# Reordering the first loads and the start of the weight loads in a linear-attention and soft-mixture kernel

## The chip, the core and the metric

The kernel runs on one core of a Trainium2 chip. The metric is the time on the device in microseconds (us); the median of several runs is given. A profile of one execution stands beside it; its span is shorter than the measured time by some 2 us, since it begins with the first instruction.

## What is computed

A linear attention with decay (batch 4, 8 heads, sequence 768, head width 48), whose output goes through a soft mixture of 8 experts with 4 slots each.

```python
state = np.zeros((B, H, D, D))
for t in range(S):
    kt, vt, rt = k[:, :, t], v[:, :, t], r[:, :, t]
    cur = einsum('bhd,bhe->bhde', u[None] * kt, vt)
    y[:, :, t] = einsum('bhd,bhde->bhe', rt, state + cur)
    state = w[None, :, :, None] * state + einsum('bhd,bhe->bhde', kt, vt)
x = y.transpose(0, 2, 1, 3).reshape(B * S, H * D)      # 3072 x 384

logits = x @ phi                                        # phi: 384 x 32
d = exp(logits - logits.max(0)); d /= d.sum(0) + 1e-9   # over the tokens
slot_input = (d.T @ x).reshape(E, 4, 384)
for e in range(8):
    slot_out[e] = relu(slot_input[e] @ w1[e]) @ w2[e]   # 384x1024, 1024x384
c = exp(logits - logits.max(1)); c /= c.sum(1) + 1e-9   # over the slots
out = c @ slot_out.reshape(32, 384)
```

Everything arrives and leaves as float32. r, k and v have 4.7 MB each, the expert weights 25.2 MB together, the output 4.7 MB.

## The kernel before

The attention works in chunks of 128 positions. A loop over `i` from -5 to 31 runs over half sequences of pairs of heads, as a software pipeline: in one pass different stages belong to different pairs. The decay is applied by powers of `w`, made from `Ln` and `Exp` on ScalarE out of one row, `w_row`.

The loads of r, k and v go through the queue of the sync engine (SP), in the order of the program:

```python
O(dve.memset(wu[:], 1.0))
O(sp.dma_start(out=w_row, in_=w.rearrange("(o h) d -> o (h d)", o=1)))
O(act.preload_act_table_set("natural_log_exp_and_others"))
O(act.dma_start(out=wu3[0:4, :, 0:D], in_=...))   # w again, for the transposed form
O(act.dma_start(out=wu3[4:8, :, 0:D], in_=...))   # u
...
load_batch(0, 2)          # k, r, v of two heads at a time, through SP
load_batch(1, 2)
O(sp.dma_start(out=phi_f, in_=...))
load_batch(2, H)          # k, r, v of all heads at a time
...
def spread(bank, a, z):   # w_row to all partitions by TensorE, then its logarithm
    O(pe.matmul(bank[:, 0:z - a], one_f, w_row[:, a:z], start=True, stop=True))
    O(act.activation(out=lnw[:, a:z], in_=bank[:, 0:z - a], func=AF.Ln))
```

There are three raw buffers for four batches; the fourth batch takes the buffer of the first, and its loads stand in the loop at `i == 3`. The expert weights go through GpSimd's queue, which also turns them from float32 into bfloat16 on the way. The `w1` have a buffer of their own, the `w2` take the raw buffers of the second and third batch once these are read. GpSimd also makes the products of k and r with the powers of the decay (`scale`). The loads of the weights are dealt over the loop; the first of them stands behind a small copy, `guard`, that reads the last batch's k and so keeps the weights behind it:

```python
W_AT = {13: 1, 14: 1, 15: 1, 16: 1, 18: 1, 19: 1, 20: 1, 22: 1, 23: 1, 25: 1, 26: 5}
for i in range(-5, nH):
    ...                                            # TensorE, VectorE, ScalarE stages
    if odd and 0 <= mu + 3 < nU:
        scale(mu + 3, 0)                           # GpSimd: k times decay
    if not odd and 0 <= mu + 2 < nU:
        scale(mu + 2, 1)                           # GpSimd: r times decay
    ...
    if i == 3:
        load_kr(0, k, B - 1, 0, H)                 # last batch
        load_kr(1, r, B - 1, 0, H)
        for h0 in range(0, H, 2):
            load_v(B - 1, h0, h0 + 2)
    if i == 5:
        O(act.copy(phi_b[:], phi_f))
    ...
    if i == min(W_AT):
        O(pool.tensor_copy(guard[:], raw_of(0, B - 1)[:, 0:1]))
    for _ in range(W_AT.get(i, 0)):
        load_w(nw)                                 # w1 of expert 0..7, then w2
        nw += 1
for y0, y1 in ((0, 4), (4, 6), (6, 8)):            # the last w2 in three pieces of rows
    load_w(nw, y0, y1)
```

After the loop the slots' inputs go through both layers of the experts. The second layer works expert by expert at its end and, within an expert, row by row, so that it can begin with the pieces of the last `w2` that are there:

```python
def second(g, experts):
    for y in range(nF):                            # 8 rows
        for x in range(2):
            for j in experts:
                O(pe.matmul(SO[x][32 * j:32 * j + 32, :], hT[g][:, y, 32 * j:32 * j + 32],
                            w2_of(g * EG + j)[:, y, x * HD:(x + 1) * HD], ...))
...
second(1, (EG - 2,))
second(1, (EG - 1,))                               # the last expert
row_sums(8, 12)
so = cst.tile([128, Dm], bf, name="so")            # slot outputs, divided by the sums
...                                                # out = c @ so, in 24 tiles, and the stores
```

Of the kernel before, what the change touches and what calls it, by code (L numbers as in the profile page):

```python
# [9 lines left out]
def kernel(  # L10
# [16 lines left out]
    Nn, Dm = out.shape  # L27
    ES = moe_phi.shape[1]
    E = moe_w1.shape[0]
    F = moe_w1.shape[2]  # L30
    Spe = ES // E
    nM = Dm // C
# [14 lines left out]
    bf = mybir.dt.bfloat16  # L47
# [4 lines left out]
    def O(ins):  # L52
        return tc.keep_in_program_order(ins)

    pe, dve, act, pool, sp = nc.tensor, nc.vector, nc.scalar, nc.gpsimd, nc.sync

    big = ctx.enter_context(tc.tile_pool(name="big", bufs=1))
    cst = ctx.enter_context(tc.tile_pool(name="cst", bufs=1))
# [36 lines left out]
    w_row = early[0:1, 0:H * D]  # L95
# [5 lines left out]
    phi_f = late[:, 128:128 + nM * ES]  # L101
    wu = cst.tile([8, 128], f32, name="wu")
    wu3 = wu[:].rearrange("q (e s) -> q e s", s=64)
    O(dve.memset(wu[:], 1.0))
    O(sp.dma_start(out=w_row, in_=w.rearrange("(o h) d -> o (h d)", o=1)))
    O(act.preload_act_table_set("natural_log_exp_and_others"))
    O(act.dma_start(out=wu3[0:4, :, 0:D], in_=w.rearrange("(q e) d -> q e d", e=2)))
    O(act.dma_start(out=wu3[4:8, :, 0:D], in_=u.rearrange("(q e) d -> q e d", e=2)))
# [104 lines left out]
    ones = cst.tile([128, 128], bf, name="ones")  # L213
    Le_t = [cst.tile([128, L, 128], bf, name=f"Le{j}") for j in range(2)]
    phi_s = cst.tile([128, nM, ES], bf, name="phi_s")
    phi_b = cst.tile([128, nM * ES], bf, name="phi_b")
    assert JV == nM
    acc = cst.tile([128, NA], f32, name="acc")
    guard = cst.tile([128, 1], f32, name="guard")
    st = {}  # L220

# [56 lines left out]
    def v_pe(i):  # L278
        m, b, q, g, n = at(i)
        vb = st["vb", m]  # L280
        for c in range(L):
            for j in range(JV):
                o = C * c - j + JV - 1
                O(pe.matmul(Vb[:, c * P2:(c + 1) * P2], Q3[:, o:o + C], vb[:, :, g, j, :],  # L284
                            start=(j == 0), stop=(j == JV - 1)))
# [6 lines left out]
    def a_pe(i):  # L292
        m, b, q, g, n = at(i)
        kT, rT = st["kT", m], st["rT", m]
        for c in range(L):
            t = slice((g * L + c) * C, (g * L + c + 1) * C)
            for e in range(2):
                s = slice(64 * e, 64 * e + 64)
                O(pe.matmul(Ab[:, e, c * C:(c + 1) * C], kT[s, t], rT[s, t]))  # L299

    def mask_f(i):
        AT = wk.tile([128, 2, L, C], bf, name="AT", bufs=2)
        st["AT", i] = AT
        O(dve.tensor_mul(AT[:], Ab[:, :, 0:T].rearrange("p e (c t) -> p e c t", c=L),  # L304
                         mask_ut[:, None, None, :].to_broadcast([128, 2, L, C])))
# [62 lines left out]
    def y_evac(i):  # L368
        m, b, q, g, n = at(i)
        if q == 0:  # L370
            st["x", n] = wk.tile([128, L, Dm], bf, name="x", bufs=4)
        O(act.copy(st["x", n][:, :, q * P2:(q + 1) * P2],  # L372
                   Yb[:, 0:L * P2].rearrange("p (c e) -> p c e", c=L)))
# [31 lines left out]
    def le_t(n, lp=None):  # L405
        Le = st["Le", n]
        lp = le_p if lp is None else lp
        for c in range(L):
            O(pe.transpose(lp[:, c * C:(c + 1) * C], Le[:, c, :], ident[:]))

    def let_ev(n, lp=None, eng=None):
        lp = le_p if lp is None else lp
        if eng is dve:
            O(dve.tensor_copy(LexpT[:, n * T:(n + 1) * T], lp))
        else:
            O(act.copy(LexpT[:, n * T:(n + 1) * T], lp))

    def disp(n, ds_p, first=True):
        x, Le = st["x", n], st["Le", n]
        for mi in range(nM):  # L420
            for c in range(L):
                O(pe.matmul(ds_p[:, mi * ES:(mi + 1) * ES].rearrange("p (j x) -> p j x", j=EG), x[:, c, mi:Dm:nM],
                            Le[:, c, :].rearrange("p (j x) -> p j x", x=32)[:, :, 0:2 * Spe],
                            start=(first and mi == 0 and c == 0), stop=(c == L - 1), skip_group_check=True))
        for c in range(L):
            O(pe.matmul(ds_p[:, NA - 1:NA], Le[:, c, :], ones[:, 0:1],
                        start=False, stop=(c == L - 1), skip_group_check=True))

    def disp_ev(n, ds_p):
        if n == 0:  # L430
            O(dve.tensor_copy(acc[:], ds_p))
        else:
            O(dve.tensor_add(acc[:], acc[:], ds_p))
# [28 lines left out]
            xt_ev(*ch[s])  # L462

    pend = []
    W_AT = {13: 1, 14: 1, 15: 1, 16: 1, 18: 1, 19: 1, 20: 1, 22: 1, 23: 1, 25: 1, 26: 5}
    T_AT = {-4: [(tt, 0, 1), (tt, 1, 1), (ex, 0, 1), (tt, 0, 2)], -3: [(ex, 1, 1), (ex, 0, 2)],
            -1: [(tt, 1, 2), (ex, 1, 2)], 0: [(tt, 0, 3), (ex, 0, 3)], 1: [(tt, 1, 3), (ex, 1, 3)]}
    Z_AT = {-3: 0, -1: 1, 1: 2, 2: 3}
# [2 lines left out]
    Wf = [t[:].rearrange("p q j d -> p (q j d)") for t in W]  # L471
# [3 lines left out]
    def turn(n, blocks, bank, eng):  # L475
        x, w_ = st["x", n], L * len(blocks) * C
        for b, mi in enumerate(blocks):
            for c in range(L):
                o = (b * L + c) * C
                O(pe.transpose(bank[:, o:o + C], x[:, c, mi * C:(mi + 1) * C], ident[:]))  # L480
        dst = xs[:, n - n0, blocks[0]:blocks[-1] + 1].rearrange("p m c t -> p (m c t)")
        if eng is dve:
            O(dve.tensor_copy(dst, bank[:, 0:w_]))
        else:
            O(act.copy(dst, bank[:, 0:w_]))
# [8 lines left out]
    for i in range(-5, nH):  # L494
        mu, odd = divmod(i, 2)
        if 0 <= i + 1 < nH:
            a_pe(i + 1)
            mask_f(i + 1)
        if pend:
            disp_ev(*pend.pop())  # L500
        if i == nH - 1:
            turn(n0, (2,), Vb[:].bitcast(bf), act)
            disp(n0 - 1, ds_t)
            le_t(n0 - 1)
            let_ev(n0 - 1, None, dve)
        if 0 <= i < nH:
            y_pe(i)
            y_evac(i)
        if 0 <= i + 2 < nH:
            v_pe(i + 2)  # L510
            v_evac(i + 2)
        if 0 <= i + 1 < nH:
            m_pe(i + 1)
            z_evac(i + 1)
        if odd == 0 and 0 <= mu + 1 < nU:
            prod_f(mu + 1)
        if odd and i > 0 and mu + 2 < nU:
            b_pe(mu + 2)
            b_evac(mu + 2)
        if odd and 0 <= mu + 3 < nU:  # L520
            scale(mu + 3, 0)
        if not odd and 0 <= mu + 2 < nU:
            scale(mu + 2, 1)
        route(i, 0)
        if 0 <= mu + 2 < nU:
            t_pe(mu + 2, odd)
            route(i, 1)
            t_evac(mu + 2, odd)
            if odd and i < 0:
                b_pe(mu + 2)  # L530
                b_evac(mu + 2)
        else:
            route(i, 1)
        if odd == 0 and 0 <= mu + 2 < nU:
            v_cast(mu + 2)
        route(i, 2)
        if i == nH - 3:
            turn(n0, (0, 1), T0, act)
        if i == nH - 2:
            turn(n1, (0, 1), T1, act)  # L540
        for f, j, q in T_AT.get(i, ()):
            f(j, q)
        if i in (-4, -3):
            wu_steps(i + 4)
        if i in Z_AT:
            q = Z_AT[i]
            O(act.activation(out=zt[:, q, 2, :], in_=zt[:, q, 0, :], func=AF.Copy, scale=wT[:, q:q + 1]))
        if i == 2:
            O(pool.memset(ones[:], 1.0))
            for t in Le_t:  # L550
                O(pool.memset(t[:], 0.0))
        if i == 3:
            load_kr(0, k, B - 1, 0, H)
            load_kr(1, r, B - 1, 0, H)
            for h0 in range(0, H, 2):
                load_v(B - 1, h0, h0 + 2)
        if i == 5:
            O(act.copy(phi_b[:], phi_f))
        if i == 6:
            for mi in range(nM):  # L560
                for j in range(nM):
                    o = C * mi - j + nM - 1
                    O(pe.matmul(Xb[:, mi * ES:(mi + 1) * ES].rearrange("p (j g s) -> p j g s", g=2, s=Spe),
                                Q3[:, o:o + C],
                                phi_b[:, j * ES:(j + 1) * ES].rearrange("p (g j s) -> p j g s", g=2, s=Spe),
                                start=(j == 0), stop=(j == nM - 1)))
            O(act.copy(phi_s[:].rearrange("p m s -> p (m s)"), Xb[:, 0:nM * ES]))
        if i == 28:
            O(pool.memset(uns, 0.0))
# [3 lines that stand above are left out]
            load_w(nw)  # L573
            nw += 1
    assert nw == 2 * E - 1
    for y0, y1 in ((0, 4), (4, 6), (6, 8)):
        load_w(nw, y0, y1)


# [87 lines left out]
    second(1, (EG - 2,))  # L667
    second(1, (EG - 1,))
    row_sums(8, 12)
    so = cst.tile([128, Dm], bf, name="so")  # L670
    O(dve.tensor_scalar_mul(so[:, 0:HD], SO[0], csr[:, 0:1]))
    O(act.activation(out=so[:, HD:Dm], in_=SO[1], func=AF.Copy, scale=csr[:, 0:1]))
    row_recip(8, 12)
# [61 lines left out]
```

The softmax here doesn't subtract the row's maximum and nothing guards it: scores larger than these inputs give would overflow.

## Time and profile before

| | |
|---|---|
| time, median of 3 runs | 122.53 us (122.38 to 122.79) |
| span of the profiled execution | 120.5 us |
| TensorE, VectorE, ScalarE, GpSimd busy | 85%, 80%, 69%, 50% |
| read from HBM, written | 39.38 MB, 4.72 MB |
| share of the 16 DMA engines' time: weight queue (GpSimd), load and store queue (SP) | 55.5%, 41.3% |
| granted TensorE clock | 0.97 |

The profile calls the engines PE (TensorE matmuls), PEld (its weight loads), DVE (VectorE), ACT (ScalarE), POOL (GpSimd) and SP (sync); a name with q is the engine's queue, where transfers are issued. L138 is line 138 of the kernel. The page divides the span into 40 slices of 3.01 us and gives one digit to each: 9 is 90% or more of the slice. In a timeline a line holds the start, the duration, the engine, the line, the operation with its output and inputs, and the count. In a table of windows a line holds the window, its length, the busy time and count of PE, PEld, DVE, ACT and POOL, the granted clock, the DMA share and the GB/s. The DMA share can exceed 1[...]. Bytes are counted as written, so a weight, read as float32 and written as bfloat16, counts half of what is read. The chain is the work that ended last, followed back from the end; here in order of time, with start and duration.

### The profile page before, as it was taken

How to read it: one execution, taken by the hardware profiler on the slowest of the kernel's cores; microseconds unless marked ns; L12 is line 12 of the kernel's file. 1: busy time of each engine (PE TensorE's matmuls, PEld its weight loads, DVE VectorE, ACT ScalarE, POOL GpSimd, SP SyncE). 2: the span in 40 equal slices, each digit the busy share in tenths (PEclk: the TensorE clock that was granted, in tenths of full speed). 3: DMA queues.
4: the chain of work that ended last, by engine and by line, in shares of the span. 5: the costliest groups of instructions: out<-in, count | busy, mean ns of one | idle time of the engine just before them, and what ended most of it. 6: DMA issues, size and time to landing. Idle time of an engine off the chain costs nothing.

```text
span 120.5 us, 4334 instructions
## 1 busy us (share of the span) xinstructions
PE 102.6 (85%) x1795; PEld 82.9 (69%) x1797; DVE 96.4 (80%) x187; ACT 83.7 (69%) x183; POOL 59.7 (50%) x70
## 2 busy tenths in 40 slices
PE   5996977799999999999999999999979996796000
PEld 1465866687887988898888898888866686583000
DVE  6899999999999999899999899999943510399000
ACT  4459769797978998888898988997963510299000
POOL 7349534599999999797677593101000000012000
PEclk9999999999999999999999999999999999999755
DMA  2999999999999999999999999999999998069992
GB/s 38 322 362 373 374 367 371 364 391 362 330 380 382 323 204 216 218 213 212 220 206 222 211 220 209 215 215 215 224 208 220 208 206 165 16 261 389 396 420 100
DMA packets 20925, 31.79 MB, mean 264 GB/s; under 512 B 1129, under 2 KB 18026, under 8 KB 20906
## 3 DMA queue, kind: packets, MB, share of 16 engines
q0 software_dynamic: 2960, 14.55, 55.5%
q1 hardware_dynamic: 17922, 16.96, 41.3%
q8 instruction: 14, 0.23, 0.7%
q14 instruction: 5, 0.04, 0.1%
q10 hardware_dynamic: 24, 0.00, 0.0%
HBM read 39.38 MB, written 4.72 MB: 366 GB/s over the span
## 4 chain that ended last, share of the span: by engine, by line
PE 37%; DMA 31%; DVE 15%; issue 6%; ACT 1%; POOL 1%; POOLq 0%; DVEq 0%; ACTq 0%
DMA raw<-in_moe_w_dram 31%; PE Vb L284 5%; PE T L235 4%; PE Ab L299 4%; PE Yb L352 3%; DVE W L188 3%; PE T L247 2%; PE Mb L325 2%; DVE prod L257 2%; PE Yb L365 2%; DVE kn L252 2%; DVE Z L341 2%; PE Xb L387 2%; PE Xb L380 2%; PE Yb L144 2%
## 5 line engine op out<-in xcount | busy, mean ns | idle before, releaser
L228 POOL TENSOR_TENSOR kr<-raw,W 128x576 bf16<-128x576 f32 x30 | 42.2, 1426 | 12.4 <-PE T L235 5.2
L304 DVE TENSOR_TENSOR AT<-Ab,mask_ut 128x768 bf16<-128x768 f32 x32 | 30.2, 945 | 0.8 <-PE Ab L299 0.6
L284 PE MATMUL Vb<-v_bf,Q 128*128 128x96 bf16 x288 | 18.2, 211 | 0.0
L235 PE MATMUL T<-ident,kr 128*128 128x128 bf16 x192 | 17.2, 230 | 1.0 <-POOL kr L228 1.0
L284 PEld LDWEIGHTS <-Q 128*128 128x128 bf16 x288 | 16.3, 100 | 1.5 <-issue 0.2
L241 ACT COPY kT<-T 128x768 bf16<-128x768 bf16 x16 | 12.8, 799 | 4.6 <-PE T L235 3.3
L241 ACT COPY rT<-T 128x768 bf16<-128x768 bf16 x16 | 12.8, 800 | 4.2 <-PE T L235 3.6
L257 DVE TENSOR_TENSOR prod<-T,kT 128x768 bf16<-128x768 bf16 x16 | 15.2, 947 | 0.0
L342 DVE TENSOR_TENSOR dv<-vn,Mb 128x288 bf16<-128x288 bf16 x32 | 14.1, 440 | 0.0
L235 PEld LDWEIGHTS <-kr 128*128 128x128 bf16 x192 | 12.7, 102 | 1.8 <-POOL kr L228 1.2
L290 ACT CAST vn<-Vb 128x288 bf16<-128x288 f32 x32 | 13.4, 419 | 0.1
L372 ACT CAST x<-Yb 128x288 bf16<-128x288 f32 x32 | 13.1, 409 | 0.2 <-PE Yb L365 0.2
L341 DVE TENSOR_TENSOR Z<-Mb,zt 128x288 bf16<-128x288 f32 (+1 forms) x32 | 12.7, 395 | 0.6
L299 PE MATMUL Ab<-rT,kT 64*128 64x128 bf16 x192 | 11.1, 222 | 2.1 <-DVE AT L304 2.1
L704 POOL DMA_DIRECT2D out_dram<-W x1 | 0.5, 549 | 24.9 <-DVE W L686 24.9
L325 PE MATMUL Mb<-vn,kn 128*128 128x96 bf16 (+2 forms) x80 | 11.5, 242 | 0.0
L352 PE MATMUL Yb<-vn,AT 128*128 128x48 bf16 x192 | 10.3, 185 | 0.1
L270 ACT CAST v_bf<-raw 128x576 bf16<-128x576 f32 x15 | 10.2, 677 | 0.0
L299 PEld LDWEIGHTS <-kT 64*128 64x128 bf16 x192 | 5.6, 95 | 5.6 <-DVE AT L304 2.0
L138 POOL DMA_DIRECT2D raw<-in_moe_w_dram x10 | 5.5, 557 | 7.9 <-DMA raw<-in_moe_w_dram 6.5
L352 PEld LDWEIGHTS <-AT 128*128 128x128 bf16 x192 | 7.1, 96 | 3.3
L365 PE MATMUL Yb<-dv,ident 128*128 128x288 bf16 x32 | 9.1, 285 | 0.2
(143 smaller groups left out, 221.7 us busy)
## 6 DMA issues: line engine op xcount, KB each, us to landing
w_all<-in_moe_w_dram POOLq DMA_DIRECT2D x8, 768.0 KB, 12.7
raw<-in_moe_w_dram POOLq DMA_DIRECT2D x7, 768.0 KB, 18.4
raw<-in_v_dram SPq DMA_DIRECT2D x12, 288.0 KB, 6.2
raw<-in_k_dram SPq DMA_DIRECT2D x8, 288.0 KB, 6.1
raw<-in_r_dram SPq DMA_DIRECT2D x8, 288.0 KB, 5.9
raw<-in_k_dram SPq DMA_DIRECT2D x2, 1152.0 KB, 12.9
raw<-in_r_dram SPq DMA_DIRECT2D x2, 1152.0 KB, 10.3
out_dram<-raw POOLq DMA_DIRECT2D x2, 768.0 KB, 6.8
```

What stands on the lines that cost most here:

```text
L228: O(eng.tensor_mul(kr[:, j].rearrange("p j (h s) -> p j h s", s=64)[:, :, :, 0:D], src, W[j][:, q].rearrange("p j (h d) -> p j h d", h=2)))
L235: O(pe.transpose(bank[:, x * C:(x + 1) * C], kr[:, j, x, :], ident[:]))
L241: O(act.copy(t[:].rearrange("p (s j) -> p s j", j=J), bank[:, 0:S].rearrange("p (j s) -> p s j", j=J)))
L257: O(dve.tensor_mul(pr[:].rearrange("p (s j) -> p s j", j=J), T1[:, 0:S].rearrange("p (j s) -> p s j", j=J), st["kT", m][:].rearrange("p (s ...
L284: O(pe.matmul(Vb[:, c * P2:(c + 1) * P2], Q3[:, o:o + C], vb[:, :, g, j, :], start=(j == 0), stop=(j == JV - 1)))
L290: O(act.copy(vn[:].rearrange("p c e d -> p (c e d)"), Vb[:, 0:L * P2]))
L299: O(pe.matmul(Ab[:, e, c * C:(c + 1) * C], kT[s, t], rT[s, t]))
L304: O(dve.tensor_mul(AT[:], Ab[:, :, 0:T].rearrange("p e (c t) -> p e c t", c=L), mask_ut[:, None, None, :].to_broadcast([128, 2, L, C])))
L325: O(pe.matmul(o, kn[:, g * L + c, :], vc, start=first, stop=True, skip_group_check=True))
L341: O(dve.tensor_mul(Z[:], Mb[:, 0:x * P2].rearrange("p (c e) -> p c e", c=x), zt[:, q, 0:x, :]))
L342: O(dve.tensor_mul(dv[:], st["v", i][:].rearrange("p c e d -> p (c e) d"), Mb[:, 288:288 + 2 * L, None].to_broadcast([128, L * 2, D])))
L352: O(pe.matmul(Yb[:, o:o + D], AT[:, e, c, :], vn[:, c, e, :], start=first, stop=False, skip_group_check=True))
```

## The change

The first three parts aim at the stream of transfers, the last makes room in the on-chip memory.

- The row of w is loaded through ScalarE's queue instead of SP's, so that the first k is the first transfer in SP's queue.
- The guard, which waits for the last batch's k, and the first weight behind it stand at `i == 12` instead of 13; of the ten weights dealt singly, the first five stand an iteration sooner.
- The last weight's pieces are of 4, 3 and 1 rows instead of 4, 2 and 2, so that fewer matmuls stand behind the last piece.
- `phi_b` takes the memory of `acc`, which is written only later, and `so` a part of the second decay buffer that isn't used any more by then. No operation is added or removed by this.

```diff
-    O(sp.dma_start(out=w_row, in_=w.rearrange("(o h) d -> o (h d)", o=1)))
+    O(act.dma_start(out=w_row, in_=w.rearrange("(o h) d -> o (h d)", o=1)))
     O(act.preload_act_table_set("natural_log_exp_and_others"))
 ...
-    phi_b = cst.tile([128, nM * ES], bf, name="phi_b")
     acc = cst.tile([128, NA], f32, name="acc")
+    phi_b = acc[:].bitcast(bf)[:, 0:nM * ES]
 ...
-    W_AT = {13: 1, 14: 1, 15: 1, 16: 1, 18: 1, 19: 1, 20: 1, 22: 1, 23: 1, 25: 1, 26: 5}
+    W_AT = {12: 1, 13: 1, 14: 1, 15: 1, 17: 1, 19: 1, 20: 1, 22: 1, 23: 1, 25: 1, 26: 5}
 ...
-            O(act.copy(phi_b[:], phi_f))
+            O(act.copy(phi_b, phi_f))
 ...
-    for y0, y1 in ((0, 4), (4, 6), (6, 8)):
+    for y0, y1 in ((0, 4), (4, 7), (7, 8)):
         load_w(nw, y0, y1)
 ...
-    so = cst.tile([128, Dm], bf, name="so")
+    so = Wf[1].bitcast(bf)[:, 2 * F + nM * ES * 8:2 * F + nM * ES * 8 + Dm]
```

## The prediction

> **What bounds the kernel now.** I read the page from the top: busy shares, the 40 slices, the queues, the chain; then the timeline of the issuing queues, and the DMA in fine windows.
>
> ```profile
> PE 102.6 (85%) x1795; PEld 82.9 (69%) x1797; DVE 96.4 (80%) x187; ACT 83.7 (69%) x183; POOL 59.7 (50%) x70
> ...
> DMA  2999999999999999999999999999999998069992
> ...
> PE 37%; DMA 31%; DVE 15%; issue 6%; ACT 1%; POOL 1%; POOLq 0%; DVEq 0%; ACTq 0%
> ```
>
> TensorE has the largest share, yet it isn't what ends late. The DMA row is at 9 from the second slice to the 33rd, about 3 to 99 us, without a hole. The chain, in order of time, says how the end is reached:
>
> ```profile
> 66.26 15.18 DMA raw<-in_moe_w_dram
> ...
> 81.97 21.82 DMA raw<-in_moe_w_dram
> 103.79 0.04 issue
> 103.83 0.24 PE Xb L660
> 104.08 0.08 PE Yb L660
> 104.16 0.10 PE Xb L660
> ```
>
> From 66 to 104 us it is nearly all weights landing. The last piece, issued at 81.97, lands at about 103.8; four matmuls follow, and then a fixed tail (output projection and stores) to 120.5. How far was the compute ahead? TensorE finished everything that didn't need the last two experts at 99.02. Each expert then costs 16 matmuls at 0.083 us (the step between starts of L660), 1.3 us; without waits it would have ended at about 99.0 + 2.7 = 101.7, against 104.2. **So the bound is one DMA stream with no idle stretch**, and the compute has some 2.5 us to spare at its end. A change gains by what it takes out of that stream: a later start than needed, a gap within, or work after its last byte. The windows show the speeds of the stages:
>
> ```profile
> 36.00:41.00 5.00, 5.00 (x101) 4.21 (x100) 5.00 (x11) 4.19 (x11) 4.98 (x7) 1.00 1.10 371
> 41.00:43.00 2.00, 1.98 (x43) 1.66 (x40) 2.00 (x4) 2.00 (x5) 1.98 (x3) 1.00 1.08 237
> 43.00:60.00 17.00, 16.88 (x348) 14.56 (x346) 16.48 (x32) 14.82 (x35) 14.40 (x14) 1.00 1.04 215
> ```
>
> The last two columns are the DMA share and GB/s of bytes written. k, r and v come at 371; the weights are halved to bf16 on the way, so their 215 is 430 GB/s read. Both stages are full. The seam, 41 to 43, is where I look for a gap, since a share above 1 there only says that packets were open, not that they moved.
>
> **What the Trainium skill says.** (1) "DMA: Bandwidth & Descriptors", section "Issuing engines are not separate DMA queues": transfers of different issuers run on the same 16 DMA engines, and another issuer saves only sequencer time. So moving w is worth at most one issue. The trace agrees that an issue is small: 0.34 us for w. (2) "Perfetto Trace Analysis", section "DMA Instruction — HWDGE (DVE, Sync)": the descriptor generator is locked by one issuer at a time, and the reported issue time includes the wait for that lock. In the trace ScalarE's first small issue takes 1.24 us beside two from SP, where SP's own w took 0.34: it agrees. (3) "DMA: Bandwidth & Descriptors", section "Anatomy of one DMA — SWDGE (gpsimd) path": about 2 us of each such transfer are fixed. The first weight here takes 2.5 us from issue to a full stream (below). (4) "ScalarE: Activation LUTs", section "What ACT_TABLE_LOAD costs": about 1.28 us; the trace shows 1.28 us, at 0.73.
>
> **The change part by part.**
>
> k first. The start of SP's queue now:
>
> ```profile
> 0.74 0.34 SPq L105 DMA_DIRECT2D LexpT<-in_w_dram  x1
> 1.14 0.41 SPq L115 DMA_DIRECT2D raw<-in_k_dram  x1
> 1.60 0.46 SPq L115 DMA_DIRECT2D raw<-in_r_dram  x1
> ```
>
> Without w the first k can issue at 0.74 and not 1.14, 0.40 us sooner, and the stream behind it has no hole in which that could be lost: each 288 KB takes 0.8 us at 371 GB/s but 0.5 us to issue. Yet ScalarE now asks for the generator at the same moment. If w wins the lock, k gets little. I take 0.3 us of the 0.40. The price is on w: its landing isn't in the trace, but TensorE's spreading of it starts at 3.13, and the decay powers follow through Ln and Exp to the first scaled k at 5.94. A w up to 0.5 us later delays that by as much. It doesn't set the end as long as the 2.5 us of spare aren't eaten. The table load now stands after one issue; the first Ln runs at 3.91, so even 1.2 us later (about 3.2) it is in time.
>
> Weights and guard an iteration sooner. GpSimd, around the guard:
>
> ```profile
> 40.09 0.20 POOL L571 COPY guard<-raw 128x1 f32<-128x1 f32 x1
> 40.22 0.75 POOL L135 DMA_DIRECT2D w_all<-in_moe_w_dram  x1
> 40.98 1.42 POOL L228 TENSOR_TENSOR kr<-raw,W 128x576 bf16<-128x576 f32 x1
> 42.35 0.59 POOL L135 DMA_DIRECT2D w_all<-in_moe_w_dram  x1
> ```
>
> An iteration on GpSimd here is one kr product, 1.37 us, so the guard goes to about 38.7 and the first weight's issue to about 38.85. Does the guard then wait for k? The last k was issued at 24.41 and landed 12.9 us later, at 37.3, and with k first some 0.3 sooner: 1.4 us of margin, no wait. What does an earlier weight bring? The queue split between 41.25 and 43.00 gives it: 456 packets of the hardware queue, 576 B each, 0.26 MB, worth 0.70 us at 371 GB/s; and 23 packets of the weight queue, 0.14 MB written, worth 0.66 us at 215. That is 1.36 us of work in 1.75 us: **0.39 us lost**. The cause is visible too: the weight was issued at 40.22, only 12 of its packets ran before 42.75, and then 11 came within 0.25 us. Started 1.37 us sooner, its queue is full at about 41.4, before the last v drains. I take 0.35 us, since k first moves the drain forward by 0.3 as well, which eats some of the lead. The four more weights that move by an iteration only lengthen a queue that is already deep: a weight takes 15 to 28 us to land where moving it takes about 3.7.
>
> The last piece of one row. Pieces are now 4, 2 and 2 rows; they become 4, 3 and 1. The bytes are the same, so the last landing stays. After it 2 matmuls stand instead of 4, 2 x 0.083 = 0.17 us less. But the middle piece now has 6 matmuls, 0.50 us. The middle and last pieces landed 0.90 us apart for two rows; one row makes it about 0.45. So those 6 end some 0.05 to 0.1 us after the last landing. Net gain about 0.1 us.
>
> The two aliases. phi_b in acc is read in iteration 6, acc first written at the first dispatch, in iteration 13. so in the second W tile lies at columns where nothing else lives by then. No instruction is added; I give them 0.
>
> Sum: 0.3 + 0.35 + 0.1 = 0.75 us. 122.53 - 0.75 = **121.8 us**.
>
> **The rivals.**
>
> *The guard becomes a wait.* If the last k lands later than I read it, GpSimd stands there with kr products behind it, and TensorE, 95% or more busy there, would soon starve. For it: weights' and k's issues are closer now. Against it: 1.4 us of margin, and GpSimd is ahead by up to three kr buffers (from 49 us it waits for TensorE, not the other way round). Should it wait 1 us, the compute's spare takes it: still about 122.
>
> *The last v starves behind the weights.* Both queues now share the engines for longer, and weight packets are ten times as large. v would land at perhaps 45 or 50 and not 42 to 44. Its first use is the cast of the last batch's first heads on ScalarE, the fourth from last of the fifteen, at 65.8. It would have to be over 20 us late to matter. Bytes are only reordered: no change of the time; in a bad case, with compute held up by several us, 123 to 124.
>
> *The start is lost on the lock.* w takes the generator first, k gains nothing, and w too lands no sooner. Then only the seam and the tail pay: 122.1.
>
> *The transfer was hidden anyway.* The batches' slots could hold the stream: the last k waits until its slot is read. GpSimd's last read of it ends at 24.25, and SP's issue of that k begins at 24.41 with 2 MB or more still queued, so the slot isn't the limit. If compute started later through w, the slot would free at about 24.7 and the queue still wouldn't run dry.
>
> **Range and chances.** Full gain of every part: 0.40 + 0.39 + 0.17 = 0.96, 121.6. None: 122.5. The stream's speed itself may shift by some tenths of a per cent of about 100 us when queues mix, so I widen to 121.1 and 122.6. A gain of over 2% needs 2.45 us, more than twice all I can find; a loss of that size needs one of the first two rivals at its worst. Chances: faster 0.03, same 0.95, slower 0.02.
>
> **What would show each step.** First k issue at about 0.75, and the DMA reaching full share about 0.3 us before the present 3.0; ScalarE's issue of w longer than 0.34. The guard at about 38.7 with no wait ahead of it, the first weight's issue near 38.9, and GB/s that go from about 370 to 215 without the stretch of under 180. The last landing near 103.1 where it is 103.8, and two matmuls after it. The stores' tail unchanged at about 16 us. I am wrong if the guard shows a wait, if the compute reaches the last experts after their weights have landed, or if the stream starts earlier and ends at the same time, which would mean that the engines, not the queue's start, set the last landing.

## The result and the profile after

The changed kernel takes 121.61 us (median of 4 runs, 121.52 to 121.83) against 122.48 us before: ratio 0.9927, 95% interval 0.9904 to 0.9950, 0.9 us less. A second measurement on another occasion gave 0.9910 (0.9893 to 0.9928), 1.1 us less. The predicted 121.8 us and its range hold; the parts of the sum don't hold as well, as the experiments show. The range of 121.1 to 122.6 us also takes in a gain of nothing, so that it holds says little by itself.

The chain of waits after the change, in order of time (start, duration, what). It answers to the chain before, where the last piece landed at about 103.8 and four matmuls followed:

```profile
61.56 15.75 DMA raw<-in_moe_w_dram
...
77.84 24.80 DMA raw<-in_moe_w_dram
102.64 0.04 issue
102.68 0.24 PE Xb L660
102.92 0.08 PE Yb L660
103.00 0.08 PE Xb L660
```

It is still weights landing up to the end. Two things differ. The piece that TensorE waits for is now the middle one, issued at 77.84 and landed at 102.64; the last one, of one row, was issued at 81.91 and took 21.2 us, so it landed at 103.09, while the six matmuls of the middle piece still ran. And the matmuls end earlier: the next instruction on TensorE, the row sums of L637, begins at 103.43 where it began at 104.25 (before, then after; the last line is the landing of the last piece after):

```profile
104.25 0.44 PE L637 MATMUL Mb<-ones,LexpT 128*128 128x1 bf16 x4
103.43 0.44 PE L637 MATMUL Mb<-ones,LexpT 128*128 128x1 bf16 x4
raw<-in_moe_w_dram POOLq DMA_DIRECT2D x1, 96.0 KB, 21.2
```

So the gain of these two profiles has two parts: the last landing comes 0.70 us sooner (103.09 for 103.79), and the work between it and the row sums shrinks from 0.46 to 0.34 us. From the row sums to the end the two kernels are alike (16.4 and 16.3 us).

SP's queue and GpSimd's, from the timeline of the changed kernel (start, duration, engine, line, what):

```profile
0.74 0.44 SPq L115 DMA_DIRECT2D raw<-in_k_dram  x1
1.23 0.46 SPq L115 DMA_DIRECT2D raw<-in_r_dram  x1
...
4.72 0.90 SPq L115 DMA_DIRECT2D raw<-in_r_dram  x1
6.47 0.37 SPq L119 DMA_DIRECT2D raw<-in_v_dram  x1
```

```profile
25.10 13.72 POOL L228 TENSOR_TENSOR kr<-raw,W 128x576 bf16<-128x576 f32 x10
38.76 0.20 POOL L571 COPY guard<-raw 128x1 f32<-128x1 f32 x1
38.88 0.75 POOL L135 DMA_DIRECT2D w_all<-in_moe_w_dram  x1
```

The first k goes at 0.74 as foretold, but a hole in SP's issues from 5.62 to 6.47 is new. The guard stands at 38.76, straight behind the product before it, without a wait.

The seam between the two queues, in the table of windows of the changed kernel (the last two columns are the DMA share and the GB/s written):

```profile
36.00:41.00 5.00, 5.00 (x102) 4.21 (x101) 5.00 (x11) 4.21 (x10) 4.98 (x6) 1.00 1.11 370
41.00:43.00 2.00, 1.98 (x42) 1.65 (x43) 2.00 (x4) 1.97 (x5) 1.98 (x4) 1.00 1.18 293
43.00:60.00 17.00, 16.87 (x347) 14.55 (x345) 16.48 (x32) 14.87 (x35) 14.37 (x15) 1.00 1.04 215
```

The stages to both sides are as fast as before (371 and 215 there); between them 237 GB/s have become 293. Of the queues' packets from 41.25 to 43.00 us, before and then after:

```profile
q0 software_dynamic: 23, 0.14, 61.0%
q1 hardware_dynamic: 456, 0.25, 47.3%
```

```profile
q0 software_dynamic: 40, 0.25, 70.1%
q1 hardware_dynamic: 468, 0.26, 49.9%
```

The columns are packets, MB and share of the 16 engines; q0 is the weights' queue, q1 that of the loads. Priced as in the prediction, 0.26 MB at 371 GB/s and 0.25 MB at 215 are 1.86 us of work in 1.75 us, where it was 1.36 us (with 0.26 MB, 456 packets of 576 B): the loss is gone, and some 0.5 us more work is done in the same window. That more is priced than the window holds shows an error of at least 0.1 us in this way of pricing.

### The profile page after: what moved, and what is told of

Same layout as the page of the kernel before. It is cut to its first block, busy times and chain, and to the rows that moved or that the text cites. A ratio compares the mean times of both kernels' runs of the same rounds, so it can differ in the third digit from the quotient of the medians.

```text
span 119.8 us, 4336 instructions
## 1 busy us (share of the span) xinstructions
PE 102.0 (85%) x1797; PEld 82.0 (68%) x1797; DVE 96.4 (81%) x187; ACT 83.9 (70%) x183; POOL 59.2 (49%) x70
## 4 chain that ended last, share of the span: by engine, by line
DMA 34%; PE 28%; DVE 17%; issue 6%; ACT 3%; POOL 3%; POOLq 0%; DVEq 0%; ACTq 0%
DMA raw<-in_moe_w_dram 34%; PE Vb L284 4%; PE T L235 3%; DVE W L188 3%; DVE prod L257 3%; PE Ab L299 3%; PE Yb L352 2%; POOL kr L228 2%; DVE AT L304 2%; PE T L247 2%; PE Mb L325 2%; DVE kn L252 2%; DVE Z L341 2%; PE Yb L144 2%; PE Yb L365 1%
```

## The experiments

All ratios are against the kernel before, run beside each on the same chip; 0.1% is 0.12 us.

### Each part alone

```diff
# kfirst
-    O(sp.dma_start(out=w_row, ...))
+    O(act.dma_start(out=w_row, ...))
# wearly
-    W_AT = {13: 1, 14: 1, 15: 1, 16: 1, 18: 1, 19: 1, ...}
+    W_AT = {12: 1, 13: 1, 14: 1, 15: 1, 17: 1, 19: 1, ...}
# pieces
-    for y0, y1 in ((0, 4), (4, 6), (6, 8)):
+    for y0, y1 in ((0, 4), (4, 7), (7, 8)):
# alias: phi_b in acc, so in the second decay buffer
```

k first, expected:

> The kernel before with one edit: the row of w through ScalarE's queue, so that k is first in SP's. Theory A (the prediction's): the whole stream starts 0.3 us sooner and nothing behind it can lose that, so the time falls by 0.3 us (0.2 to 0.4). Theory B (from the trace after the change): SP's ninth load now waits for the landing of the first v, because transfers of both queues share eight completion semaphores in turn and the turn has shifted; SP issues nothing from 5.6 to 6.4 us, and by 7 us no more bytes have moved than before. Then the first k issues at 0.74, but the time is unchanged within 0.1 us.

Measured: ratio 0.9999 (0.9984 to 1.0015). No difference, and 0.3 us lies outside the interval. It is a sign that the prediction named for being wrong: the stream starts earlier and ends at the same time. The bytes of the first microseconds say where the lead goes. Windows of 2 us of the kernel before, then of this one:

```profile
2.00:4.00 2.00, 2.00 (x6) 1.02 (x5) 1.93 (x8) 0.10 (x2) 1.88 (x5) 1.00 0.83 246
4.00:6.00 2.00, 2.00 (x5) 0.49 (x5) 1.67 (x5) 1.24 (x4) 0.09 (x1) 1.00 0.99 290
```

```profile
2.00:4.00 2.00, 2.00 (x6) 1.02 (x5) 1.93 (x6) 0.67 (x2) 1.88 (x5) 1.00 1.00 297
4.00:6.00 2.00, 2.00 (x5) 0.48 (x5) 1.78 (x9) 1.24 (x4) 0.07 (x1) 1.00 0.97 244
```

51 GB/s more from 2 to 4 us, 46 less from 4 to 6: the lead of about 0.1 MB is given back at once. The other profiles mostly agree. By 8 us the six without k first have moved 1.77 to 1.82 MB and the eight with it 1.72 to 1.95; only two of the eight (1.89 and 1.95) are clearly ahead.

In this profile the stream also sagged to 248 GB/s from 22 to 24 us and was late for the seam, yet the end didn't move: 13.72 MB moved by 41 us where it was 13.95, but 18.03 by 60 us where it was 18.08. The seam gave back most of the delay. That fits a first weight that is issued by GpSimd's clock (40.22 in both) and not when the loads before it are done: loads that come later fill the gap, and loads that come sooner would widen it. The table of windows shows 315 GB/s in this seam, without any gain: a fast seam alone isn't a gain, if what fills it is late.

The weights' start, expected:

> The kernel before with one edit: the guard and the first five weights an iteration sooner. Theory A: it fills the seam between v and the weights, 0.35 us of the prediction. Theory B (the bytes moved from 38 to 46 us in the two traces, 0.11 MB more, worth 0.5 us at 215 GB/s): this part alone brings 0.5 to 0.7 us, nearly the whole difference. Both: the guard at about 38.7 with no wait before it. A rival in which the guard waits for k would show an idle stretch of GpSimd ahead of it.

Measured: 0.9963 (0.9945 to 0.9981), 0.45 us less. The guard ran at 38.72 without a wait, and the seam rose from 237 to 284 GB/s:

```profile
41.00:43.00 2.00, 1.98 (x43) 1.65 (x40) 2.00 (x4) 2.00 (x5) 1.98 (x4) 1.00 1.15 284
```

This part alone is clear of the noise; it was run once more below, with the same outcome. The weights' packets in the window from 41.25 to 43.00 us tell the two starts apart: 14 to 23 in the four profiles with the guard at 13, 35 to 44 in the eight with it at 12.

The pieces, and the aliases, expected:

> The kernel before with one edit: the last weight in pieces of 4, 3 and 1 rows. The prediction: 0.1 us less, from two matmuls fewer behind the last landing, less what the middle piece's six add. The trace after the change, where TensorE's last wait is on the middle piece and eight matmuls follow it without a wait: 0.1 to 0.15 us less. A rival: the small piece slows the last landing, and nothing is gained.

> The kernel before with the two aliases alone (phi_b in acc, so in the second decay buffer). No operation is added or removed: 0, within 0.1 us. A rival: a wait on the shared buffers in the output stage, which would lengthen the stretch from the last weight matmul to the end (16.3 us before).

Measured: 0.9998 (0.9982 to 1.0014) and 1.0006 (0.9991 to 1.0021). Neither shows a difference by itself in time. With the pieces, too, TensorE's last wait is on the middle piece, at 103.79, and eight matmuls follow. The traces have the size of this part all the same: from the last landing to the row sums it is 0.46 us in each of the seven profiles with the old pieces and 0.30 to 0.34 in six with the new ones (noguard9, below, left aside). That is 0.12 to 0.16 us less work behind the last byte, too little for the interval of the times to show. With the aliases the stretch after the last weight matmul is as long as before.

The four parts alone sum to 0.4 us, with an uncertainty of about as much; the whole gives 0.9 to 1.1. The next runs ask for what comes only in company.

### The parts in company

```diff
# after_p42: the changed kernel with the old pieces
-    for y0, y1 in ((0, 4), (4, 7), (7, 8)):
+    for y0, y1 in ((0, 4), (4, 6), (6, 8)):
# after_wsp: the changed kernel with w ahead of k in SP's queue again
-    O(act.dma_start(out=w_row, ...))
+    O(sp.dma_start(out=w_row, ...))
# wearly_kfirst: the kernel before with those two edits alone
```

> The changed kernel itself, for comparison on the same chip. If the parts add (start 0, weights 0.4 to 0.6, pieces 0, aliases 0), 0.4 to 0.6 us less than before. If the start or the pieces pay only together with earlier weights, the 0.9 us of the first measurement come back.

> The changed kernel with the last weight again in pieces of 4, 2 and 2 rows. In the trace of the changed kernel the middle piece landed 0.47 us before the last, and its six matmuls ended as the last landed. Prediction's theory: 0.1 us slower than the changed kernel. Rival (pieces alone made no difference): the same time within 0.1 us.

> The kernel before with the weights' start alone, once more, for the comparison with the next two on one chip: 0.3 to 0.6 us less than before.

> The kernel before with k first and the weights' start, without the pieces and the aliases. Alone, k first brought 0.0 and the start of the weights 0.45 us. Theory F: alone it can't bring anything, since the weights start by GpSimd's clock (40.2 us) and a stream of k, r and v that ends sooner only widens the seam; with the weights ready sooner it brings what is left of its 0.4 us after the slow stretch from 4 to 6 us, 0.1 to 0.3 us more than the weights' start alone. Theory G: the whole lead is lost in the slow stretch; the same as the weights' start alone within 0.1 us.

> The changed kernel with w again through SP's queue, ahead of k. The changed kernel is 1.1 us below before, its parts alone sum to 0.4. Theory F: without k first 0.1 to 0.3 us of that go. Theory G: the time of the changed kernel within 0.1 us, and the rest of the 1.1 us comes from the pieces in company with the earlier weights.

| kernel | median, us | ratio | 95% interval |
|---|---|---|---|
| changed kernel again | 121.64 | 0.9910 | 0.9893 to 0.9928 |
| without the pieces (after_p42) | 121.83 | 0.9936 | 0.9916 to 0.9956 |
| without k first (after_wsp) | 121.95 | 0.9945 | 0.9927 to 0.9963 |
| weights' start and k first (wearly_kfirst) | 121.81 | 0.9937 | 0.9916 to 0.9959 |
| weights' start alone, again (wearly_again) | 122.16 | 0.9955 | 0.9938 to 0.9971 |

The weights' start is confirmed at 0.4 to 0.6 us. Taking k first away from the changed kernel costs 0.35% (0.9945 less 0.9910), adding it to the weights' start brings 0.18%; taking the pieces away costs 0.26%. So by the times both are worth some 0.2 to 0.4 us here and 0.0 alone, which is what theory F expects of k first. But each of these differences has an uncertainty of about 0.26%, from the two intervals, so only the first is clear of zero, and it compares two chip sessions (against the first measurement of the changed kernel it would be 0.18%). For the pieces the traces give 0.12 to 0.16 us, here as alone, so company isn't needed. That k first pays in company isn't settled, and the profiles don't show it: with the guard at 12 they have moved 18.16 and 18.22 MB by 60 us without k first, and 18.17 to 18.24 with it (18.02 to 18.09 with the guard at 13). Left aside is the profile of the weights' start again, of a run of 123.40 us in which the stream sagged to 253 GB/s from 22 to 24 us.

### What eats the lead of k first

```diff
# after_wu_pool: the changed kernel with
-    O(act.dma_start(out=wu3[0:4, ...], ...))
-    O(act.dma_start(out=wu3[4:8, ...], ...))
+    O(pool.dma_start(out=wu3[0:4, ...], ...))
+    O(pool.dma_start(out=wu3[4:8, ...], ...))
```

> The changed kernel with the two small loads into wu moved from ScalarE's queue to GpSimd's. These then take no turn among the eight completion semaphores that SP's and ScalarE's loads share, so SP's ninth load waits for the first k (landed by 3.8 us) and not for the first v (6.4 us); and ScalarE asks for the descriptor generator once and not three times. Theory B (the shifted turn ate what k first would bring): SP's issues run on past 5.6 us without the 0.85 us hole, the stream is 0.2 to 0.3 us ahead at 20 us, and the time falls by 0.2 to 0.3 us against the changed kernel. Rival C (the slow stretch from 4 to 6 us, which every trace has, is not made by the issues): the hole in SP's issues goes, the bytes moved by 7 us stay at 1.4 MB, and the time stays within 0.1 us.

Measured: 0.9947 (0.9928 to 0.9966), 122.02 us, 0.4 us slower than the changed kernel beside it, with single runs from 121.15 to 122.94. Theory B, my own from the hole in SP's issues, falls. The hole is gone, and the slow stretch isn't:

```profile
5.49 0.47 SPq L119 DMA_DIRECT2D raw<-in_v_dram  x1
6.00 0.94 SPq L115 DMA_DIRECT2D raw<-in_k_dram  x1
```

```profile
4.00:6.00 2.00, 2.00 (x5) 0.48 (x5) 2.00 (x6) 1.22 (x3) 1.88 (x5) 1.00 0.94 252
```

So the issues and the turn of the semaphores don't make the sag from 4 to 6 us. It is in every profile, 207 to 298 GB/s in those with k first and 269 to 308 in those without, with the engines open nearly all the time (share 0.92 to 1.07), and its depth differs from run to run of the same kernel: 207 in one profile of the changed kernel, 298 in the next. What makes it stays open. Why this variant is slower than the changed kernel was not found either.

### How early may the weights start

```diff
# guard11
-    W_AT = {12: 1, 13: 1, 14: 1, 15: 1, 17: 1, 19: 1, ...}
+    W_AT = {11: 1, 12: 1, 13: 1, 14: 1, 16: 1, 19: 1, ...}
# noguard9
-    W_AT = {12: 1, 13: 1, 14: 1, 15: 1, 17: 1, 19: 1, ...}
+    W_AT = {9: 1, 10: 1, 11: 1, 12: 1, 14: 1, 19: 1, ...}
-    O(pool.tensor_copy(guard[:], raw_of(0, B - 1)[:, 0:1]))
```

> The changed kernel without the guard copy and with the first five weights dealt at iterations 9, 10, 11, 12, 14 (first issue about 34.7 us). Theory D: an engine turns to the weight queue only as its hardware queue runs dry, as in four traces the first weight packets ran at 41 to 42 us whether the first issue was at 38.9 or 40.2; then packets of weights still begin near 41 us, the seam is as closed as before and the time is the same within 0.1 us. Theory E (the queues share in turn): weight packets run from about 37 us, k, r and v land later by some us, the bytes in all stay the same and so does the time, or it grows by up to 1 us if the last k or r come too late for GpSimd (needed at about 51 us).

Measured: 143.38 us, ratio 1.1658 (1.1632 to 1.1683), 20 us slower. Theory D is false and theory E was far too mild. The first weight was issued at 34.84 and its packets ran from about 38.7. From then on the last v starved. The queues from 50 to 54 us (packets, MB, share of the engines), and ScalarE's longest wait:

```profile
q0 software_dynamic: 144, 0.79, 94.8%
q1 hardware_dynamic: 145, 0.08, 9.1%
```

```profile
ACT v_bf L270 <- DMA raw<-in_v_dram: 20.0, 3, 11.7
```

One packet for one: 144 of the weights against 145 of v, and so on from 40 to 78 us. A weight's packet has 5.5 KB, one of v 576 B, so v gets a tenth of the bytes. Its last four pieces, of two heads each, land at 57.9, 72.3, 88.2 and 101.6 us; their casts begin at 65.99, 72.29, 88.27 and 101.59, the third after 11.7 us of waiting, the fourth after 6.9. The compute hangs on it, and in the slices from 102 to 127 us, with the weights all in, the DMA stands nearly idle. The run moves the start and leaves out the guard at once, so it doesn't say what a guard at 9 would do.

> The changed kernel with the guard and the first five weights a further iteration sooner (11), first issue near 37.5 us if the guard doesn't wait for k, which lands near 37.0. With the guard out and the start at 9 the last v starved, one small packet of it for each large one of the weights, 143 each in 4 us, and ScalarE waited 20 us for it. Here about 0.5 MB of v, 900 packets, are left when weight packets begin near 40.3; at 36 packets in a us they last till about 65 us, and v is needed from 65.8 to 79.8 us. So: the same time as the changed kernel within 0.2 us, with v packets running until 55 to 65 us. Rival: the last pieces of v come late and ScalarE's casts wait, then 1 us or more slower.

Measured: 0.9956 (0.9941 to 0.9971), 122.18 us, single runs from 121.43 to 122.95. The guard ran at 37.88, without a wait. The last v trickled until 62.3 us in the same way:

```profile
q0 software_dynamic: 142, 0.78, 94.4%
q1 hardware_dynamic: 143, 0.08, 9.2%
```

(from 46 to 50 us). No cast waited for them, as reckoned; still it is 0.5 us slower than the changed kernel, though the comparison is across chips. Its last landing comes at 103.76 in the profile, those of the changed kernel at 103.03 and 103.09; why was not found. So iteration 12 is the best start of those tried: at 13 there is a seam, at 11 some of the gain is gone, and too early with no guard is a cliff.

## Why the prediction was right, point by point

- **The bound.** That one DMA stream sets the end held in every run but one: what made the weights land sooner made the kernel faster by about as much. The last landing moved by 0.70 us, the work behind it shrank by 0.12, and the end of the matmuls moved by their sum, 0.82.
- **Guard and weights' start.** The mechanism and the instants held: guard at 38.76 (38.7 predicted), no wait. The term was a little small: 0.35 us against 0.45 and 0.55 alone, and some 0.5 us more work in the window. I had taken something off because k first was to move the drain forward, and k first didn't. The first packet moved less than the issue: it ran at about 41.5 and not 41.7, and at 41.1 in the run of this part alone, though the issue was 1.3 us sooner; what grew is the number of packets that followed.
- **Two readings beside it** were off. The 15 to 28 us to land are those of the later weights, the `w2`; the `w1`, of which the first five were moved, land in 6.9 to 15.8 us, still longer than the 3.7 us of moving one. And the 2.5 us from issue to a full stream aren't the fixed part that the prediction takes from the Trainium skill, "DMA: Bandwidth & Descriptors", section "Anatomy of one DMA — SWDGE (gpsimd) path": that section puts most of its 2 us behind the last byte, and the 1.4 to 3.9 us seen here lie ahead of the first packet.
- **k first.** The issue at 0.74 was right, the step from there was wrong: "the stream behind it has no hole in which that could be lost". There are two places. The stretch from 4 to 6 us, which the trace of before already showed (290 GB/s where 370 is usual) and which I passed over, swallows most of the lead; and the first weight is issued by GpSimd's clock, so loads that end sooner would only meet a wider seam. 0.3 us were predicted; alone it is 0.0, and in company it stays open between 0.0 and 0.4.
- **The lock.** ScalarE's issue of w took 0.53 us beside SP's first k, against 0.34 on SP, as expected of two issuers at a time; TensorE's spreading of w began at 3.13 in both kernels, so w was no later where it counts.
- **The pieces.** The middle and last landing stand 0.45 us apart, as predicted, and the six matmuls end just after the last landing, as worked out. 0.1 us was predicted and 0.12 to 0.16 us is what the traces show; the times, 0.0 alone with an uncertainty of 0.2 and 0.3 in company with one of 0.3, agree with it and don't settle it.
- **The rivals.** The starving v is real, and a start at 9 without the guard costs 20 us, where my bad case for this change was "123 to 124". It doesn't strike at iteration 12: some 0.2 MB of v are left when the weights' packets begin, where it was 0.5 MB with the start at 11, and the last of it lands at 44.7 us (43.7 before). The waiting guard didn't occur.
- **The sum** came out at 0.75 against 0.9 and 1.1 partly by luck: the term of k first was too large, and the two others were too small.

## What to carry to other kernels

When two queues follow each other and DMA is the bound, price the seam between them in bytes per queue against time; a DMA share near 1 hides it (here 1.08 with 0.4 us lost), and so does a high rate whose bytes are only late. Moving the start of one queue closes a seam only where its start is what opens it; a lead ahead of a queue that starts by another engine's clock may buy nothing. And before letting a queue of large packets start earlier, see what small packets it will share the engines with and when these are needed.

## What the runs showed of the hardware that was not expected

- Two queues on the same engines, both with packets waiting, shared them packet for packet, 144 to 145 in 4 us, not by bytes: 0.79 MB to 0.08 MB.
- A weight's transfer took 2.6 us (38.88 to about 41.5) and 3.9 us (34.84 to about 38.7) from issue to its first packet while the other queue was full, and 1.4 us (40.22 to about 41.7) when that was about to drain.
- The stream of loads sags to between 207 and 298 GB/s from 4 to 6 us after the start in the profiles with k first (269 to 308 in the others), and in two profiles of different kernels again from 22 to 24 us (248 and 253 GB/s); neither was explained.
